# Q, K and V of five of eight pairs of column groups from seven block products in place of eight

## The chip, the cores and the metric

The kernel runs on one core of a Trainium2 chip. The metric is the device time of one execution in microseconds. Five engines work at once, each in its own order: TensorE (PE, matmuls; its weight loads, PEld, overlap them), VectorE (DVE), ScalarE (ACT), GpSimd (POOL) and SyncE (SP, which issues most of the transfers). Matmuls write to PSUM, whose banks DVE and ACT read.

## The reference

One transformer block with two parallel branches on a normalized input, S = 2048 rows of D = 576, hidden size F = 4608, H = 32 heads of 18:

```python
xn = _layernorm(x, axis=-1)
return x + _A_ref(xn, A_wqkv, A_wo) + _B_ref(xn, B_w1, B_b1, B_w2, B_b2)
```

`_A_ref` computes q, k and v = xn @ wqkv, attends from each position to the 8 positions at distance 0, 2, ..., 14 behind it (softmax over those that exist), and multiplies by wo. `_B_ref` is a feed-forward network: h = relu(xn @ w1 + b1), squared, times w2, plus b2.

## The kernel before

The rows are cut into NB = 4 blocks of TB = 512. All matmuls take F32R operands. For accuracy each operand is split into a rounded part (hi) and the remainder (lo), and hi·hi, hi·lo and lo·hi are summed in PSUM. D = 576 is four chunks of 128 and a last one of 64; the last chunk's hi and lo lie on top of each other in one fifth tile of 128 partitions, so it needs two matmuls and not three.

The work is written out in steps. There are NT = 144, 36 in each block, one for each slice of 128 of F. Step n loads the weights of slice n + 2 (`load_w`), splits w1 of slice n + 1 (`split_w1`: an ACT copy L118 to w1h, a DVE subtraction L120 to w1l), runs what `pre` lists for the step, then `ffn1(n)` (14 matmuls L492 of 512 columns into a bank of PSUM; Relu L494 and two Squares L497 and L498 on ACT, the remainder hl on DVE L499), `split_w2(n)` (L124, L126), what `mid` lists, two pieces of side work, `ffn2(n - 2)` (14 matmuls L515 into five banks that stay open for the whole block), and a third piece. The order in which an engine's instructions really stand is chosen at build time by a scheduler that works through the program in that order of priority; only the opening and the tail are written by hand (`manual_schedule`). `issue_after` puts what an engine gets in its block behind a given instruction of that engine.

Q, K and V of a block are made in four groups of columns (8 heads each: 144 columns of K, 144 of V, and some of Q). In blocks 1 to 3 the groups have 512, 512, 384 and 320 columns (`WIDE`), in block 0 448, 512, 384 and 384; always 1728 in all. `load_wq` loads a group's five chunks of weights and splits them (L118, L120, 10 instructions on each of two tiles `wqh`, `wql`). `qkv` then runs, for each of NJ = 4 slices of 128 rows, 14 matmuls (`three`, L372; in block 0's first group L236) into a bank `wk` of which there are three, and copies Q, K and V out with three ACT copies (L393 to L395). `qkv_close` sends K and V to memory and gets the 14 rows before the block back. Matmuls L372 have the x part as the stationary and the weights as the moving operand.

`attention(b, g)` is side work on DVE in 19 pieces (products L425 and L447, sums L428 and L451 to L453, small operations L435 to L442), then a write to memory and a gather (`ob`). `o_chunk` and `o_acc` in steps 29 to 37 of a block transpose the result and multiply it by wo into the open banks; they need all four groups. `layernorm` (statistics L138, a power on POOL L147) and `normalize` (L334 and a split) prepare the next block's x, which `load_x` has loaded in two layouts, rows (`xb`) and transposed (`xt`). `load_residual` loads x again (`xr`), to which `finish` adds the open banks at a block's end. In before, block b's four groups start in steps -2, 4, 11 and 18 of the block (9, 15 and 20 in block 0), with their weights three or four steps earlier. All loads and stores but the opening's two are issued by SP.

Of the kernel before, what the change touches and what calls it, by code (L numbers as in the profile page):

```python
# [43 lines left out]
def block_kernel(ctx: ExitStack, tc: tile.TileContext, x, xt, wqkv, wo, w1, b1, w2, b2, out):  # L44
# [5 lines left out]
    pw = ctx.enter_context(tc.tile_pool(name="pw", bufs=3, space=bass.MemoryType.PSUM))  # L50
# [39 lines left out]
    yp = {}  # L90

    def load_x(b):
        xb[b] = sb.tile([P, NJ, D], F32, name="xb", bufs=1)
        with tc.issue_after(last_load[0].ins):
            nc.sync.dma_start(xb[b], xv[b])
            xT[b] = sb.tile([P, NC, TB], F32, name="xt", bufs=1)
            nc.sync.dma_start(xT[b], xt[b])

    def load_first():
        xb[0] = sb.tile([P, NJ, D], F32, name="xb", bufs=1)  # L100
        raw = sb.tile([P, NC, TB], F32, name="xr", bufs=1)[:, :, :WIDE[0][0]]
        hi = mt.tile([P, NC, WQ], F32R, name="wqh")[:, :, :WIDE[0][0]]
        lo = mt.tile([P, NC, WQ], F32R, name="wql")[:, :, :WIDE[0][0]]
        nc.sync.dma_start(xb[0][:, 0, :288], xv[0, :, 0, :288])  # L104
        nc.scalar.dma_start(xb[0][:, 0, 288:], xv[0, :, 0, 288:])
        nc.scalar.dma_start(raw[:, 0], wqkv[0, 0, :, 0, :WIDE[0][0]])
        nc.sync.dma_start(xb[0][:, 1], xv[0, :, 1])
        for c in range(1, NC):
            nc.sync.dma_start(raw[:, c], wqkv[0, 0, :, c, :WIDE[0][0]])
# [19 lines left out]
    ln, last_load, last_hl = {}, [None], [None]  # L129
# [61 lines left out]
    def open_rows():  # L191
# [36 lines left out]
        def part(j, i):  # L228
# [3 lines left out]
            if (0, j) not in qp:  # L232
                qp[0, j] = pw.tile([P, TB], F32, name="wk")
                done[j] = 0
            done[j] += 1
            nc.tensor.matmul(qp[0, j][:, :WIDE[0][0]], (xl if a == 1 else xh)[0][:, c, js], (lo if a == 2 else hi)[:, c],  # L236
# [109 lines left out]
    def load_residual(b):  # L346
        xr[b] = sb.tile([P, NC, TB], F32, name="xr", bufs=1)
        nc.sync.dma_start(xr[b][:, :NC - 1], xt[b, :, :NC - 1])
        nc.sync.dma_start(xr[b][:D - DM, NC - 1], xt[b, :D - DM, NC - 1])
# [3 lines left out]

    def load_wq(b, g):
        n = WIDE[b][g]
        hi = mt.tile([P, NC, WQ], F32R, name="wqh")[:, :, :n]
        lo = mt.tile([P, NC, WQ], F32R, name="wql")[:, :, :n]
        for c in range(NC):
            r = sb.tile([P, n], F32, name="wqr", bufs=2)
            nc.sync.dma_start(r, wqkv[min(b, 1), g, :, c, :n])  # L360
# [3 lines left out]
    kv, attended = {}, set()  # L364
# [10 lines left out]

    def qkv_open(b, g, w):
        if g == 0:
            qo[b] = sb.tile([P, NJ, D], F32, name="qo", bufs=1)
            ob[b] = sb.tile([P, NJ * G, CG], F32, name="ob", bufs=1)
# [3 lines left out]
    def qkv_rows(b, g, j):  # L383
        hi, lo = qw[g]
        p = qp[g, j] = pw.tile([P, TB], F32, name="wk")
        js = slice(j * P, (j + 1) * P)
        three(p[:, :WIDE[b][g]], lambda c: xh[b][:, c, js], lambda c: xl[b][:, c, js],
# [281 lines left out]
    def step(n):  # L669
# [21 lines left out]
        if not busy:  # L691
            piece()
# [50 lines left out]
```

## Time and profile before

| What | us |
|---|---|
| time, median of 3 runs | 1161.33 (1161.21 to 1161.37) |
| the profiled execution's own time | 1161.42 |
| its span, first to last instruction | 1159.7 |
| PE busy | 1154.3 |
| DVE busy | 847.5 |
| ACT busy | 602.2 |
| POOL busy | 18.3 |
| transfers: 185.90 MB, mean 160 GB/s, 16 engines busy | 50.4% |

A profile row for a group of instructions reads: line, engine, operation, output tile <- input tiles, shapes, xcount, then busy time in us and the mean of one in ns, then the idle time of the engine just before them and what ended it. A row by form gives shortest, median and longest duration in ns and the first and last start. A row of the chain in time, or of a timeline, begins with start and duration in us. A row of waits reads: waiting engine and line <- engine and line waited for, us in total, times, longest. A row by stretch gives its ends, its length, the busy us (and instructions) of PE, PEld, DVE, ACT and POOL, then TensorE's granted clock, the share of the DMA engines' time and GB/s. A row of transfers gives the tile, the issuing queue, the count, KB of one, and the median us from issue to landing.

### The profile page before, as it was taken

The numbers are of one execution on the slowest core, as the hardware profiler recorded it, in microseconds if no ns is written. First come the engines' busy times: TensorE is split into PE (matmuls) and PEld (weight loads), VectorE is DVE, ScalarE is ACT, GpSimd is POOL, SyncE is SP. The second block draws the span as 40 slices with busy tenths as digits, with TensorE's granted clock in tenths as the row PEclk, the third lists the DMA queues.
The fourth block names the chain that finished last, engine by engine and source line by source line (L and its number), as shares of the span: only waits on it lengthen the run. The fifth ranks groups of instructions, "written<-read, shape, count | busy, mean of one in ns | idle before, by whom it ended". The sixth has DMA issues, their size and how long they took to land.

```text
span 1159.7 us, 14795 instructions
## 1 busy us (share of the span) xinstructions
PE 1154.3 (100%) x5227; PEld 966.5 (83%) x5227; DVE 847.5 (73%) x1373; ACT 602.2 (52%) x1086; POOL 18.3 (2%) x32
## 2 busy tenths in 40 slices
PE   9999999999999999999999999999999999999998
PEld 7888888888888888888888888888888888888887
DVE  6967798892788686995287969698528795957453
ACT  7645545563545454555364546555535455545552
POOL 2000000000000100000000010000000000000000
PEclk9999999999999999999999999999999999999999
DMA  8656547432656655444266665644326645353421
GB/s 290 214 170 223 177 133 234 123 112 63 209 190 206 212 183 198 132 115 120 63 234 203 203 216 153 214 111 125 106 75 232 221 131 184 108 181 111 121 63 51
DMA packets 89674, 185.90 MB, mean 160 GB/s; under 512 B 9984, under 2 KB 33280, under 8 KB 88320
## 3 DMA queue, kind: packets, MB, share of 16 engines
q1 hardware_dynamic: 89312, 184.58, 50.1%
q8 instruction: 41, 0.67, 0.2%
q10 hardware_dynamic: 288, 0.38, 0.1%
q14 instruction: 33, 0.27, 0.1%
HBM read 165.96 MB, written 18.96 MB: 159 GB/s over the span
## 4 chain that ended last, share of the span: by engine, by line
PE 99%; DMA 0%; DVE 0%; SPq 0%; issue 0%
PE y L515 44%; PE wk L492 39%; PE wk L372 14%; PE wk L236 1%; DMA xb<-in_x 0%; PE y L172 0%; PE wk L564 0%; DVE st L138 0%; DVE xr L566 0%; SPq L104 0%; DVE xt L166 0%
## 5 line engine op out<-in xcount | busy, mean ns | idle before, releaser
L515 PE MATMUL y<-hh,w2s 128*128 128x512 f32 x1292 | 319.8, 389 | 0.0
L515 PEld LDWEIGHTS y<-hh,w2s 128*128 128x128 f32 x1292 | 242.5, 188 | 50.4
L492 PE MATMUL wk<-xh,w1h 128*128 128x512 f32 x720 | 210.3, 389 | 0.0
L515 PE MATMUL y<-hl,w2s 128*128 128x512 f32 x718 | 189.5, 389 | 0.0
L492 PE MATMUL wk<-xh,w1l 128*128 128x512 f32 x720 | 187.6, 389 | 0.0
L120 DVE TENSOR_TENSOR w1l<-raw,w1h 128x640 fp32r<-128x640 f32 x144 | 118.1, 820 | 66.4 <-ACT w1h L118 52.0
L118 ACT ACTIVATE w1h<-raw 128x640 fp32r<-128x640 f32 x144 | 106.1, 737 | 115.7 <-PE wk L492 114.0
L124 ACT ACTIVATE w2s<-raw 128x576 fp32r<-128x576 f32 x144 | 97.8, 683 | 120.0 <-PE y L515 118.1
L492 PEld LDWEIGHTS wk<-xh,w1l 128*128 128x128 f32 x720 | 135.1, 188 | 28.1
L515 PEld LDWEIGHTS y<-hl,w2s 128*128 128x128 f32 x718 | 134.8, 188 | 28.0
L492 PEld LDWEIGHTS wk<-xh,w1h 128*128 128x128 f32 x720 | 134.9, 188 | 27.5
L492 PE MATMUL wk<-xl,w1h 128*128 128x512 f32 x576 | 154.1, 389 | 0.0
L126 DVE TENSOR_TENSOR w2s<-raw,w2s 128x512 fp32r<-128x512 f32 (+1 forms) x288 | 118.0, 453 | 47.3 <-ACT w2s L124 46.2
L499 DVE TENSOR_TENSOR hl<-r,hh 128x512 fp32r<-128x512 f32 x144 | 98.8, 686 | 42.4 <-ACT r L498 42.3
L492 PEld LDWEIGHTS wk<-xl,w1h 128*128 128x128 f32 x576 | 108.1, 188 | 22.6
L494 ACT ACTIVATE r<-wk,b1t 128x512 f32<-128x512 f32 x144 | 98.5, 684 | 39.7 <-PE wk L492 39.4
L425 DVE TENSOR_TENSOR pr<-qo,kv 128x1152 f32<-128x1152 f32 x64 | 86.6, 1353 | 34.7 <-DMA kv<-kscr 34.7
L372 PE MATMUL wk<-wqh,xh 128*128 128x512 f32 (+2 forms) x300 | 106.3, 355 | 0.0
L372 PE MATMUL wk<-wql,xh 128*128 128x512 f32 (+2 forms) x300 | 106.3, 355 | 0.0
L498 ACT ACTIVATE r<-r 128x512 f32<-128x512 f32 x144 | 91.0, 632 | 4.4
L497 ACT ACTIVATE hh<-r 128x512 fp32r<-128x512 f32 x144 | 90.9, 632 | 4.1
L447 DVE TENSOR_TENSOR pr<-lg,kv 128x1152 f32<-128x1152 f32 x64 | 86.8, 1356 | 1.6
(91 smaller groups left out, 961.1 us busy)
## 6 DMA issues: line engine op xcount, KB each, us to landing
raw<-in_w SPq DMA_DIRECT2D x144, 320.0 KB, 3.0
raw<-in_w SPq DMA_DIRECT2D x144, 288.0 KB, 2.8
kv<-kscr SPq DMA_DIRECT2D x16, 1008.0 KB, 5.7
kv<-vscr SPq DMA_DIRECT2D x16, 1008.0 KB, 8.2
wqr<-in_wqkv SPq DMA_DIRECT2D x35, 256.0 KB, 3.3
raw<-in_wo SPq DMA_DIRECT2D x20, 288.0 KB, 2.8
wqr<-in_wqkv SPq DMA_DIRECT2D x25, 192.0 KB, 4.0
kscr<-kv SPq DMA_DIRECT2D x16, 288.0 KB, 3.0
```

The source lines that it names most:

```text
L118: i = nc.scalar.activation(hi, raw, AF.Copy)
L120: i = nc.vector.tensor_tensor(out=lo, in0=raw, in1=hi.bitcast(F32), op=ALU.subtract)
L124: nc.scalar.activation(w[:, :D], raw, AF.Copy)
L126: nc.vector.tensor_tensor(out=w[:, o:o + n], in0=raw[:, a:a + n], in1=w[:, a:a + n].bitcast(F32), op=ALU.subtract)
L372: nc.tensor.matmul(ps, l, r, start=i == 0, stop=i == len(mm) - 1)
L447: nc.vector.tensor_tensor(out=pr.rearrange("p w (a d) -> p w a d", d=DH), in0=at[:, :, :, None].to_broadcast([P, W, HG, DH]), in1=shifted( ...
L492: nc.tensor.matmul(p, l, r, start=i == 0, stop=i == len(mm) - 1)
L494: nc.scalar.activation(r, p, AF.Relu, bias=b1t[:, f:f + 1])
L497: nc.scalar.activation(hh, r, AF.Square)
L498: nc.scalar.activation(r, r, AF.Square)
L499: last_hl[0] = nc.vector.tensor_tensor(out=hl, in0=r, in1=hh.bitcast(F32), op=ALU.subtract)
L515: nc.tensor.matmul(yp[b][c], v, a, start=first and c not in cs[:i], stop=c in last and c not in cs[i + 1:], skip_group_check=True)
```

## The change

Groups 0 and 1 form pair 0, groups 2 and 3 pair 1; in a pair both groups now have 432 columns (`PAIR`). Block 0 is made as before. In block 1 pair 0, in blocks 2 and 3 both pairs are made with seven block products (Winograd's form of Strassen's scheme). The four full chunks make two halves of the inner dimension, the 512 rows two halves of 256, the pair's two groups two halves of the columns. A product (`multiply`) takes sums of parts of x and sums of parts of the weights over two chunks: 2 x 3 matmuls for each of two slices of 128 rows. The fifth chunk isn't part of the scheme; products 2, 7, 4 and 3 carry two more matmuls a slice for it (`EXTRA`). Products 1 and 2, products 6, 7 and 4, and products 5 and 3 each accumulate in the same two banks (`qk`); after each product its state is copied (ACT, products 1 and 2) or added to a kept result (DVE, the others): K and V to `cst`, which takes the place of `xb`, and Q to `qo`.

The sums of x for products 6, 7, 5 and 3 are made on DVE from the normalized `xT`, rounded by ACT and the remainder taken by DVE (`sums`, tile `sx`). The sums of weights are made once, pair 0's in block 0 from step 6 and pair 1's in block 1 from step 13 of the block (`preparation`): quarters of the weights are loaded through POOL's queue into `xt` and `xr` while these are free, POOL subtracts (`minus`), ACT rounds, POOL takes the remainder and stores both to memory (`emit`: 17 a pair). In block 0 one is made each step, in block 1 three in two steps. `load_product` gets one product's weights from memory two steps ahead, through POOL's queue, into `wqh` and `wql` in turn, and the fifth chunk's sums into the end of that tile and into `wqr`.

One product is made each step: pair 0 of block 1 in steps 42 to 48, of blocks 2 and 3 in steps -6 to 0 of the block, pair 1 in steps 3 to 9. In these steps `ffn1` uses the bank `wk` alone (`held`); else it goes through the three banks as before (`bank`). Groups 2 and 3 of block 1 are made as before, in steps -2 and 3 of the block, with 432 columns. `fetch` then gets a group's K and V whole from memory and starts its attention: in steps 13 and 18 of block 1, and 1, 6, 11 and 16 of blocks 2 and 3. The transposed x is loaded 14 steps ahead of a block in place of 26, the rows 25; normalization starts 12 steps ahead, or 11, and then goes before the other side work. The residual is loaded in step 34, 68, and 13 of blocks 2 and 3. From step 19 on every odd step has a fourth piece of side work.

```diff
-WIDE = [(448, 512, 384, 384)] + 3 * [(512, 512, 384, 320)]
-QAT = [[sum(n - 2 * CG for n in w[:g]) for g in range(G + 1)] for w in WIDE]
+WIDE = (448, 512, 384, 384)
+QAT = [sum(n - 2 * CG for n in WIDE[:g]) for g in range(G + 1)]
+PAIR = (432, 432)
+QP = (0, 288)
+PREP = (6, 13)
...
+    turns, held = [0], set()
+
+    def bank(own=False):
+        turns[0] += not own
+        if own or turns[0] % 3 == 0:
+            return pw.tile([P, TB], F32, name="wk")
+        return pw.tile([P, TB], F32, name="qk", bufs=2)
...
+    def load_xt(b):
+        xT[b] = sb.tile([P, NC, TB], F32, name="xt", bufs=1)
...
+    def columns(b, g):
+        if b:
+            p, h = divmod(g, 2)
+            n = PAIR[p]
+            q = QP[p] + h * (n - 2 * CG)
+            return n, q, lambda c: wpair[p, :, c, h, :n]
+        n = WIDE[g]
+        return n, QAT[g], lambda c: wqkv[g, :, c, :n]
...
+    def minus(out, a, b):
+        nc.gpsimd.tensor_tensor(out=out, in0=a, in1=b, op=ALU.subtract)
+
+    def emit(raw, dst, n):
+        outs[0] += 1
+        o = mt.tile([P, 2, n], F32R, name=("wos", "sx", "wqh", "wql")[outs[0] % (2 if outs[0] < 18 else 4)], bufs=1)
+        split(o[:, 0], o[:, 1], raw, nc.scalar)
+        minus(o[:, 1], raw, o[:, 0].bitcast(F32))
+        nc.gpsimd.dma_start(dst, o.bitcast(F32))
+
+    quarters = {}
+
+    def load_quarter(p, m, c, h):
+        n = PAIR[p]
+        if c < 4:
+            k, home = 2 * (c // 2) + h, "xt" if m == p else "xr"
+        else:
+            k, home = 4, "xr" if h else "xt"
+        if (p, home) not in quarters:
+            quarters[p, home] = sb.tile([P, NC, TB], F32, name=home, bufs=1).rearrange("p c t -> p (c t)")
+        v = quarters[p, c, h] = quarters[p, home][:, k * n:(k + 1) * n]
+        i = nc.gpsimd.tensor_copy(v[:, :1], gate[0][:, :1].bitcast(F32))
+        with tc.issue_after(i.ins):
+            nc.gpsimd.dma_start(v, wpair[p, :, c, h, :n])
+
+    def preparation(p):
+        b = lambda c, h: quarters[p, c, h]
+        n = PAIR[p]
+        for m in (p, 1 - p):
+            for i, c, h, minuend in ((1, 0, 0, None), (2, 2, 0, None), (3, 2, 1, None), (5, 0, 0, (0, 1)), (7, 0, 1, (2, 1)),
+                                     (6, 2, 1, (0, 0)), (4, 2, 0, (2, 1))):
+                c += m
+                if i == 5:
+                    minus(b(c, h), b(m, 1), b(c, h))
+                elif i == 7:
+                    minus(b(c, h), b(2 + m, 1), b(c, h))
+                elif i == 6:
+                    minus(b(c, h), b(c, h), b(m, 0))
+                elif i == 4:
+                    minus(b(c, h), b(c, h), b(2 + m, 1))
+                emit(b(c, h), wm[p][i - 1][:, 2 * m:2 * m + 2], n)
+                yield
+            if m == p:
+                for h in (1, 0):
+                    emit(b(4, h), we[p][h], n)
+                    yield
+                minus(b(4, 1), b(4, 0), b(4, 1))
+                emit(b(4, 1), we[p][2], n)
+                yield
+
+    EXTRA = {2: 0, 7: 1, 4: 2, 3: 1}
+    mw, sx, qk, cst = {}, {}, {}, {}
+
+    def load_product(b, p, i, k):
+        n = PAIR[p]
+        t = mt.tile([P, NC, WQ], F32R, name=("wqh", "wql")[k % 2]).rearrange("p c t -> p (c t)")
+        w = t[:, :4 * n].rearrange("p (c t) -> p c t", c=4)
+        nc.gpsimd.dma_start(w, wm[p][i - 1])
+        hi = lo = None
+        if i in EXTRA:
+            hi = t[:, 4 * n:5 * n]
+            lo = sb.tile([P, n], F32R, name="wqr", bufs=2)
+            nc.gpsimd.dma_start(hi, we[p][EXTRA[i]][:, 0])
+            nc.gpsimd.dma_start(lo, we[p][EXTRA[i]][:, 1])
+        mw[i] = w, hi, lo
+
+    HALF = TB // 2
+
+    def sums(b, i):
+        v = lambda k, t: xT[b][:, 2 * k:2 * k + 2, t * HALF:(t + 1) * HALF]
+        s = sx[i] = mt.tile([P, 4, HALF], F32R, name="sx")
+        lo = s[:, 2:]
+        f = sb.tile([P, TB], F32, name="r", bufs=3).rearrange("p (c t) -> p c t", c=2)
+
+        def tt(out, a, b, op):
+            nc.vector.tensor_tensor(out=out, in0=a, in1=b, op=op)
+
+        if i == 7:
+            tt(f, v(0, 0), v(0, 1), ALU.subtract)
+        else:
+            tt(f, v(0, 1), v(1, 1), ALU.add)
+            if i != 5:
+                tt(f, f, v(0, 0), ALU.subtract)
+            if i == 3:
+                tt(f, v(1, 0), f, ALU.subtract)
+        nc.scalar.activation(s[:, :2], f, AF.Copy)
+        tt(lo, f, s[:, :2].bitcast(F32), ALU.subtract)
+
+    def result(b, p, t, row, col):
+        j = 2 * row + t
+        n = PAIR[p]
+        q = QP[p] + col * (n - 2 * CG)
+        return cst[b, p][:, col, :, j], qo[b][:, j, q:q + n - 2 * CG]
+
+    def halves(a, n):
+        return a[:, :2 * CG].rearrange("p (k c) -> p k c", k=2), a[:, 2 * CG:n]
+
+    def multiply(b, p, i):
+        n = PAIR[p]
+        if i == 1:
+            cst[b, p] = sb.tile([P, 2, 2, NJ, CG], F32, name="xb", bufs=1)
+            results(b)
+        w, ehi, elo = mw.pop(i)
+        s = sx.pop(i, None)
+        first = i in (1, 6, 5)
+        for t in range(2):
+            if first:
+                qk[t] = pw.tile([P, TB], F32, name="qk", bufs=2)
+            at = slice(t * P, (t + 1) * P)
+            if s is None:
+                k, row = {1: (0, 0), 2: (1, 0), 4: (1, 1)}[i]
+                js = slice(row * HALF + t * P, row * HALF + (t + 1) * P)
+                a = lambda m: (xh[b][:, 2 * k + m, js], xl[b][:, 2 * k + m, js])
+            else:
+                a = lambda m: (s[:, m, at], s[:, 2 + m, at])
+            mm = []
+            for m in range(2):
+                hi, lo = a(m)
+                mm += [(hi, w[:, 2 * m]), (hi, w[:, 2 * m + 1]), (lo, w[:, 2 * m])]
+            if i in EXTRA:
+                row = {2: 0, 7: 1, 4: 1, 3: 0}[i]
+                js = slice(row * HALF + t * P, row * HALF + (t + 1) * P)
+                mm += [(xh[b][:, NC - 1, js], ehi), (xh[b][:, NC - 1, js], elo)]
+            for c, (l, r) in enumerate(mm):
+                nc.tensor.matmul(qk[t][:, :n], l, r, start=first and c == 0, stop=c == len(mm) - 1,
+                                 skip_group_check=True)
+        for t in range(2):
+            src = halves(qk[t], n)
+            kept = result(b, p, t, 1, 0)
+            row, col = {1: (1, 0), 2: (0, 0), 6: (0, 1), 7: (1, 1), 4: (1, 0), 5: (1, 1), 3: (0, 1)}[i]
+            for o, a, u in zip(result(b, p, t, row, col), src, kept):
+                if i in (1, 2):
+                    nc.scalar.activation(o, a, AF.Copy)
+                else:
+                    nc.vector.tensor_tensor(out=o, in0=a, in1=u if i in (6, 7, 4) else o, op=ALU.add)
+        if i in (4, 3):
+            h = (4, 3).index(i)
+            for k, scr in enumerate((kscr, vscr)):
+                nc.sync.dma_start(flat(scr[2 * p + h], (PAD + b * TB) * CG, [NJ * CG, P], NJ * CG),
+                                  cst[b, p][:, h, k].rearrange("p j c -> p (j c)"))
+
+    def fetch(b, g):
+        kv[g] = tuple(mt.tile([P, NE, CG], F32, name="kv", bufs=3) for _ in range(2))
+        for t, scr in zip(kv[g], (kscr[g], vscr[g])):
+            nc.sync.dma_start(t.rearrange("p e c -> p (e c)"),
+                              flat(scr, (PAD + b * TB - HALO) * CG, [NJ * CG, P], NE * CG))
+        side.append(attention(b, g))
...
-        p = pw.tile([P, TB], F32, name="wk")
+        p = bank(own=n in held)
...
+    prep = []
+
+    def next_difference():
+        while prep:
+            try:
+                with tc.issue_after(last_square[0].ins):
+                    next(prep[0])
+                return
+            except StopIteration:
+                prep.pop(0)
 
     def at(where, n, f, *a):
         where.setdefault(n, []).append((f, a))
...
     for b in range(NB):
         n0 = b * NF
         if b:
-            at(pre, n0 - 26, load_x, b)
+            at(pre, n0 - 25, load_x, b)
             at(pre, n0 - 22, lambda b=b: side.insert(0, layernorm(b)))
-            at(pre, n0 - 12, lambda b=b: side.append(normalize(b)))
-            at(pre, n0 - 6, load_wq, b, 0)
-        at(pre, n0 + 13, load_residual, b)
-        if b:
-            at(pre, n0 - 2, start, b, 0)
-        for g, n in ((1, 4), (2, 11), (3, 18)) if b else ((1, 9), (2, 15), (3, 20)):
-            at(pre, n0 + n - 3, load_wq, b, g)
-            at(pre, n0 + n, start, b, g)
+            at(pre, n0 - 14, load_xt, b)
+            at(pre, n0 - (12 if b < 2 else 11), lambda b=b: side.insert(0 if b > 1 else len(side), normalize(b)))
+            for p, a in enumerate((n0 - 6, n0 + 3) if b > 1 else (n0 + 6,)):
+                for k, i in enumerate((1, 2, 6, 7, 4, 5, 3)):
+                    at(pre, a + k - 2, load_product, b, p, i, k)
+                    if i in (6, 7, 5, 3):
+                        at(mid, a + k - 1, sums, b, i)
+                    at(pre, a + k, multiply, b, p, i)
+                    held.add(a + k)
+            for g, n in enumerate((1, 6, 11, 16) if b > 1 else (13, 18)):
+                at(pre, n0 + n, fetch, b, g)
+            if b < 2:
+                for g, l, n in ((2, -6, -2), (3, 1, 3)):
+                    at(pre, n0 + l, load_wq, b, g)
+                    at(pre, n0 + n, start, b, g)
+            at(pre, n0 + (13 if b > 1 else 32), load_residual, b)
+        else:
+            at(pre, 34, load_residual, b)
+            for g, n in ((1, 9), (2, 15), (3, 20)):
+                at(pre, n - 3, load_wq, b, g)
+                at(pre, n, start, b, g)
+        if b < 2:
+            a = n0 + PREP[b]
+            at(mid, a, lambda p=b: prep.append(preparation(p)))
+            when = lambda k: a + (k * 2 // 3 if b else k)
+            for k in range(17):
+                at(mid, when(k), next_difference)
+            for k, m in ((0, b), (10, 1 - b)):
+                for i, (c, h) in enumerate(((m, 0), (2 + m, 0), (2 + m, 1), (m, 1))):
+                    at(pre, when(k + i) - 3, load_quarter, b, m, c, h)
+            for i, h in enumerate((1, 0)):
+                at(pre, when(7 + i) - 3, load_quarter, b, b, NC - 1, h)
...
+            if n > 18 and n % 2:
+                piece()
```

More of the change, by code (lines that the diff above doesn't have):

```diff
@@ L90, in block_kernel @@
     yp = {}
+    turns, held = [0], set()
[4 more added lines that the diff above has]
+        return pw.tile([P, TB], F32, name="qk", bufs=2)
+    wm = [[dram.tile([P, 4, n], F32, name=f"wm{p}{i}") for i in range(7)] for p, n in enumerate(PAIR)]
+    we = [[dram.tile([P, 2, n], F32, name=f"we{p}{i}") for i in range(3)] for p, n in enumerate(PAIR)]
     def load_x(b):
@@ L384, in qkv_rows @@
         hi, lo = qw[g]
-        p = qp[g, j] = pw.tile([P, TB], F32, name="wk")
+        p = qp[g, j] = bank()
         js = slice(j * P, (j + 1) * P)
-        three(p[:, :WIDE[b][g]], lambda c: xh[b][:, c, js], lambda c: xl[b][:, c, js],
+        three(p[:, :columns(b, g)[0]], lambda c: xh[b][:, c, js], lambda c: xl[b][:, c, js],
               lambda c: hi[:, c], lambda c: lo[:, c])
@@ L577, in o_chunk @@
     def o_chunk(b, c):
-        assert b in attended
+        assert attended.count(b) == G
         if c == 0:
@@ L614, in block_kernel @@
     nc.vector.memset(warm, 0.0)
-    wp = pw.tile([P, TB], F32, name="wk")
+    wp = bank()
     def warm_up(n, width=TB, after=None):
@@ L726 @@
         "wqkv": wqkv,
+        "wpair": wpair,
         "wo": wo,
```

71 lines of the change are left out of this document (41 added, 30 removed).

## The prediction

> **What bounds the kernel now.** I read the head of the page and its chain of waits first, then the chain in order of time, then what TensorE (PE) itself waited for.
>
> ```profile
> span 1159.7 us, 14795 instructions
> PE 1154.3 (100%) x5227; PEld 966.5 (83%) x5227; DVE 847.5 (73%) x1373; ACT 602.2 (52%) x1086; POOL 18.3 (2%) x32
> PE 99%; DMA 0%; DVE 0%; SPq 0%; issue 0%
> PE y L515 44%; PE wk L492 39%; PE wk L372 14%; PE wk L236 1%; DMA xb<-in_x 0%; PE y L172 0%; PE wk L564 0%; DVE st L138 0%; DVE xr L566 0%; SPq L104 0%; DVE xt L166 0%
> 71.78 12.69 PE wk L372 x56
> 122.55 9.73 PE wk L372 x56
> 439.51 8.21 PE wk L372 x56
> 1116.15 6.35 PE y L515 x28
> PE wk L621 <- DVE warm L614: 1.2, 1, 1.2
> PE wk L619 <- POOL rs L147: 0.6, 1, 0.6
> PE y L172 <- DVE xt L166: 0.2, 1, 0.2
> ```
>
> The reader is to see one engine from end to end. The chain is 99% PE, and the last three rows are all that PE's matmuls waited for in the whole execution: 2.0 us, all in the opening. So each matmul taken out is worth its own duration, as long as no other engine or transfer becomes late. The four rows of the chain in time give that duration: 12.69/56 = 0.2266 us at 512 columns, 9.73/56 = 0.1738 at 384, 8.21/56 = 0.1466 at 320; 6.35/28 = 0.2268 in the feed-forward part, whose 28 matmuls make a step of 6.35 us. From 320 to 512 columns the price grows by 0.000417 us a column, so 432 columns cost 0.1466 + 112 x 0.000417 = 0.1933 us. By one rate for all columns it would lie between 432/512 x 0.2266 = 0.1912 and 432/384 x 0.1738 = 0.1955.
>
> **What the change removes from PE.** Two groups were 2 x 4 x 14 = 112 matmuls. A pair of them is now seven products of 2 x 6, and four of the seven carry 2 x 2 more for the fifth chunk: 84 + 16 = 100. Blocks 2 and 3 went from 56 x (2 x 0.2266 + 0.1738 + 0.1466) = 43.3 us to 200 x 0.1933 = 38.7; block 1 keeps two direct groups of 432 columns: 100 + 112 matmuls, 41.0 us. Saved: 4.66 + 4.66 + 2.33 = **11.65 us** (60 matmuls; 11.5 to 11.7 with the bounds of the price). The new order of banks adds no matmul, and the output drains and the tail aren't touched.
>
> **What it adds beside PE.** Durations are from the groups of instructions, some with shapes apart:
>
> ```profile
> L120 DVE TENSOR_TENSOR w1l<-raw,w1h 128x640 fp32r<-128x640 f32 x144 | 118.1, 820 | 66.4 <-ACT w1h L118 52.0 <-PE wk L492 11.4 <-ACT lg L438 2.6
> L126 DVE TENSOR_TENSOR w2s<-raw,w2s 128x512 fp32r<-128x512 f32 (+1 forms) x288 | 118.0, 453 | 47.3 <-ACT w2s L124 46.2
> L499 DVE TENSOR_TENSOR hl<-r,hh 128x512 fp32r<-128x512 f32 x144 | 98.8, 686 | 42.4 <-ACT r L498 42.3
> L118 ACT ACTIVATE w1h<-raw 128x640 fp32r<-128x640 f32 x144 | 106.1, 737 | 115.7 <-PE wk L492 114.0 <-DMA wqr<-in_wqkv 1.4 <-DMA raw<-in_w 0.3
> L494 ACT ACTIVATE r<-wk,b1t 128x512 f32<-128x512 f32 x144 | 98.5, 684 | 39.7 <-PE wk L492 39.4
> L447 DVE TENSOR_TENSOR pr<-lg,kv 128x1152 f32<-128x1152 f32 x64 | 86.8, 1356 | 1.6
> L425 DVE TENSOR_TENSOR pr<-qo,kv 128x1152 f32<-128x1152 f32 x64 | 86.6, 1353 | 34.7 <-DMA kv<-kscr 34.7
> L428 DVE TENSOR_REDUCE lg<-pr 128x64 f32<-128x1152 f32 x64 | 86.2, 1347 | 0.0
> L451 DVE TENSOR_TENSOR pr<-pr 128x576 f32<-128x576 f32 x64 | 48.1, 752 | 0.5
> L452 DVE TENSOR_TENSOR pr<-pr 128x288 f32<-128x288 f32 x64 | 29.1, 455 | 1.4
> L453 DVE TENSOR_TENSOR qo<-pr 128x144 f32<-128x144 f32 x64 | 19.5, 305 | 1.4
> L442 DVE TENSOR_TENSOR lg<-lg,sm 128x256 f32<-128x256 f32 x16 | 6.8, 425 | 0.6
> L441 DVE RECIPROCAL sm<-sm 128x32 f32<-128x32 f32 x16 | 5.6, 353 | 0.6
> L120 DVE TENSOR_TENSOR wql<-wqr,wqh 128x512 fp32r<-128x512 f32 (+2 forms) x75 | 44.1, 602 | 47.2 <-ACT wqh L118 47.1
> L118 ACT ACTIVATE wqh<-wqr 128x512 fp32r<-128x512 f32 (+2 forms) x75 | 40.6, 561 | 87.7 <-DMA wqr<-in_wqkv 58.1 <-PE wk L372 29.3
> L334 DVE TENSOR_TENSOR xt<-xt,mb 128x512 f32<-128x512 f32 x30 | 33.0, 1154 | 0.0
> L120 DVE TENSOR_TENSOR xl<-xt,xh 128x512 fp32r<-128x512 f32 x12 | 8.2, 710 | 0.0
> L138 DVE BATCH_NORM_STATS2 st<-xb 128x6 f32<-128x288 f32 x32 | 12.3, 447 | 10.3 <-DMA xb<-in_x 10.3
> ```
>
> VectorE (DVE), per pair: the sums of x are 11 operations of 128x512 (3 + 2 + 2 + 4), 11 x 0.686 = 7.5 us; five products are added to kept results, 5 x 2 x (0.455 + 0.305) = 7.6 us by L452 and L453. Ten splits of weights go, 10 x 44.1/75 = 5.9 us. Net 9.2 us, 46 us over five pairs: 847.5 becomes about 894 of 1150, still below PE. In a product step it fits: the 2.41 us that every step needs (0.820 + 2 x 0.453 + 0.686), 15.1/7 = 2.2 for the product, and 3.5 pieces of attention (one attention is four times the six L425 to L453 rows, 22.3, and five small operations between L441 and L442, 2.0: 24.3 us in 19 pieces, 1.28 each) make 9.05 us; PE's step is 6.35 + 14.3 x 0.1933 = 9.11. A bank is read again one step later, so its additions (1.5 us) have 6.35 us. The feed-forward part has one bank of its own in those steps, which Relu (0.684 us) must have read within the 3.17 + 2.76 us to the next use. I cost all of it at nothing; without that cover PE waits for whatever DVE or ACT is behind.
>
> ScalarE (ACT) loses more than it gains per pair (ten splits and 24 copies against eight narrower copies and four roundings) and gets 34 roundings of weights in blocks 0 and 1, 34 x 40.6/75 = 18 us: nothing, at 52% busy. They are queued behind a step's last Square, so what stands behind one that has to wait is the next weight split, which then keeps PE's next step.
>
> **The transfers.** 35 loads of 864 KB (five pairs of seven), 40 of 216 KB, and in blocks 0 and 1 54 loads and stores of quarters and sums go through POOL's queue, which carried no load before. Bounds from the SP queue:
>
> ```profile
> kv<-vscr SPq DMA_DIRECT2D x16, 1008.0 KB, 8.2
> wqr<-in_wqkv SPq DMA_DIRECT2D x15, 160.0 KB, 6.4
> xt<-in_xt SPq DMA_DIRECT2D x3, 1280.0 KB, 8.0
> ```
>
> A product's weights are issued when the product two earlier has read its buffer, and have 6.35 + 2.76 + 6.35 = 15.5 us. In parallel they need some 8 us (1,296 KB by the third row): hidden. One after the other, by the slower rows, 8.2 + 6.4 + 6.4 = 21 us: late by 5.5. I take the first end, since in all rows size adds little to a landing time of some 3 to 8 us. The two transfers moved by the change are x transposed (load_xt now two or three steps ahead of its use, 12.7 us against 8.0) and the residual (step 34 for a drain in step 37): both hidden; on SP's queue each now stands behind the feed-forward weights of its step. On POOL's queue a product's load waits for PE with only the next loads behind it, as the layer norm's powers and the subtractions fall in other steps. The K and V of the fetched groups now come whole from memory, some 8 us after the step that asks; attention starts later by that, and nothing on PE waits for its start.
>
> **The place where it is tight** is block 1, steps 49 to 66. Attention for groups 0 and 1 can't start before step 49 now, and must feed the output projection in step 67; the same steps hold layer norm and normalization of block 2, and the preparation of pair 1 on GpSimd (POOL). DVE in 17 steps: 17 x 2.41 = 41.0; two attentions 48.6; layer norm 5.4 (8 x 0.447 and small ones); normalization 15.1 (10 x 1.154, 5 x 0.710); first weights and chunk of the projection 2.3 (2 x 0.453, 2 x 0.686): 112.4 us. PE in the same steps: 17 x 6.35 = 107.9. DVE may fall behind by the lead of the next step's w1l, which PE reads 9 matmuls into it: 6.35 + 2.04 - 0.737 - 0.820 = 6.8 us. So 112.4 against 114.7: just covered, but the preparation isn't in it yet.
>
> The preparation is 26 POOL subtractions a block (17 remainders, 9 differences). The trace has two of that kind:
>
> ```profile
> L203 POOL TENSOR_TENSOR wql<-xr,wqh x2: 1147/1151/1155, 9.1 to 11.3; 128x448 fp32r<-128x448 f32 x2
> L203 DVE TENSOR_TENSOR wql<-xr,wqh x3: 618/652/967, 8.4 to 12.8; 128x448 fp32r<-128x448 f32 x3
> 9.41 0.82 DVE L138 BATCH_NORM_STATS2 st<-xb 128x6 f32<-128x288 f32 x2
> 11.26 1.16 POOL L203 TENSOR_TENSOR wql<-xr,wqh 128x448 fp32r<-128x448 f32 x1
> 11.93 1.54 DVE L203 TENSOR_TENSOR wql<-xr,wqh 128x448 fp32r<-128x448 f32 x2
> ```
>
> The first DVE operation of the last row began at 11.93, beside POOL's until 12.42 (0.49 us), and is the one of 0.967; the other two took 0.635 on average. So it lost 0.33 us of 0.49 shared. Over the two POOL operations that is 0.17 us each, and 26 x 0.17 = 4.3 us for a block: 112.4 + 4.3 - 114.7 = **2.0 us** of PE waiting in block 1. Bounds: 0, if POOL falls into DVE's gaps; 26 x 1.15 x 0.33/0.49 = 20 us lost, 18 us of waiting, if DVE always wants in. I take 2.0, since the trace has DVE work of many kinds beside POOL and only some of it slowed. In block 0 the same costs nothing by this row, even at 20 us:
>
> ```profile
> 50.00:178.00 128.00, 128.00 (x593) 109.25 (x592) 102.20 (x175) 64.35 (x128) 2.66 (x4) 1.00 0.54 171
> ```
>
> The third busy time is DVE's: 25.8 us of 128 free.
>
> **The sum.** The profiled execution took 1161.42 us (span 1159.7), 0.09 above the median of 1161.33. 1161.33 - 11.65 + 2.0 = **1151.7 us**.
>
> **The rivals.**
> *DVE locked out by POOL.* The place is block 1's preparation, the price 0.78 us of DVE for each POOL subtraction, 20 us in all; it decides against the change once DVE loses more than 14 us there (11.65 + 2.3 spare). For it: the 0.967 row, and some 80% of DVE's time (all but the reductions and layer norm) goes to operations on two tiles in SBUF, like that one. Against it: two bn_stats ran in 0.82 us beside the first POOL subtraction, against 0.447 for one on average, and POOL has idle steps in which to lag. Time: 1149.7 + 18 = 1167 us.
> The Trainium skill (SBUF — State Buffer, Who interferes with whom) states the rule behind this rival: a DVE instruction with two SBUF inputs contends with a GpSimd instruction that reads SBUF, and the later one is blocked until the first has finished. By that rule the 0.967 would have been 0.49 + 0.635 = 1.13; the row shows two thirds of it.
> *Everything is hidden.* The 6.8 us of lead and list order absorb block 1: 1149.7 us. For it: in the present trace PE doesn't wait once after the opening, though normalization comes as a burst of 15 us of DVE in two steps. Against it: no stretch now has DVE above 100% of PE, and block 1 will.
> *The weights come late.* If POOL's queue moves a product's three loads one after the other, the 20 products with a fifth chunk are each 5.5 us late: 1149.7 + 110 = 1260 us. For it: no row shows POOL's queue at such a load. Against it: the sizes and the 15.5 us.
> *It doesn't do what it says* would be PE at the old 112 matmuls a pair; the loop over products excludes it.
>
> **How the numbers follow.** The forecast, with some 1 to 7 us of waiting (1150.5 to 1156.5): 0.47. Everything hidden (1149 to 1150.5): 0.27. Locked out (1158 to 1171): 0.18, about half of it below 1165. Weights late, or additions late in product steps: 0.08. The range 1149 to 1165 holds 0.47 + 0.27 + 0.09 = 0.83. A difference under 0.2% (2.3 us) can't be told from none. Faster than 1159: the first two and a little of the third, 0.75; within 1159 to 1163.7: 0.05, from the third; slower: 0.20, the rest of the third and the fourth.
>
> **What will show it.** Right: some 60 matmuls fewer, 500 of them of 432 columns at 0.19 us; DVE near 895 us and POOL near 80; what PE waits for lies between steps 49 and 66 (400 to 520 us into the span) and names DVE. The lock: DVE operations of 0.68 us reading 1 us and more beside POOL's. Late weights: PE waiting for a DMA from the sums at the start of products. Wrong altogether: PE waits spread over blocks 2 and 3, where I count none.

## The result, and the profile after

The changed kernel took 1175.55 us (median of 4 runs, 1171.79 to 1176.26) against 1161.35 before: a ratio of 1.0116, with an interval of 1.0094 to 1.0137. It is slower, where 1151.7 was forecast. The profiled execution is the fastest of the four (1171.79 us, span 1170.1).

From its page, first busy times and the chain by engine, then the groups that answer to those of before:

```profile
span 1170.1 us, 14971 instructions
PE 1151.5 (98%) x5167; PEld 966.1 (83%) x5167; DVE 924.8 (79%) x1478; ACT 587.6 (50%) x1010; POOL 167.8 (14%) x233
PE 75%; DVE 14%; DMA 6%; issue 4%; ACT 1%; SPq 0%; POOL 0%; DVEq 0%; POOLq 0%
L136 DVE TENSOR_TENSOR w1l<-raw,w1h 128x640 fp32r<-128x640 f32 x144 | 123.9, 861 | 66.5 <-ACT w1h L134 59.1
L142 DVE TENSOR_TENSOR w2s<-raw,w2s 128x512 fp32r<-128x512 f32 (+1 forms) x288 | 125.8, 478 | 52.3 <-ACT w2s L140 51.5
L682 DVE TENSOR_TENSOR hl<-r,hh 128x512 fp32r<-128x512 f32 x144 | 107.3, 745 | 35.7 <-ACT r L681 35.7
```

The 60 matmuls are gone (5227 to 5167). But the chain, 99% PE before, is now 75% PE and 14% DVE, and the same DVE instructions on the same shapes have become longer: w1l 820 to 861 ns, hl 686 to 745 ns. A mean hides where, so here are stretches of 10 us of the changed kernel (columns: stretch, length, busy us and instructions of PE, PEld, DVE, ACT, POOL; granted clock; DMA share; GB/s) and the forms of DVE's operations between 440 and 525 us:

```profile
240.00:250.00 10.00, 8.74 (x39) 6.91 (x38) 10.00 (x15) 4.09 (x7) 0.00 (x0) 1.00 0.30 81
250.00:260.00 10.00, 7.53 (x34) 5.91 (x33) 8.49 (x16) 9.90 (x18) 0.00 (x0) 1.00 0.41 139
460.00:470.00 10.00, 8.09 (x36) 6.38 (x34) 9.93 (x8) 6.45 (x12) 9.56 (x13) 1.00 0.71 255
470.00:480.00 10.00, 8.78 (x26) 7.01 (x27) 9.93 (x11) 3.83 (x6) 3.94 (x4) 0.66 0.64 228
500.00:510.00 10.00, 7.01 (x29) 5.13 (x29) 9.90 (x12) 4.31 (x8) 5.54 (x8) 1.00 0.91 304
530.00:540.00 10.00, 8.31 (x37) 6.52 (x36) 7.75 (x13) 4.60 (x8) 0.00 (x0) 1.00 0.31 97
```

```profile
L682 DVE TENSOR_TENSOR hl<-r,hh 128x512 fp32r<-128x512 f32 x11 | 11.8, 1074 | 0.0
L142 DVE TENSOR_TENSOR w2s<-raw,w2s 128x64 fp32r<-128x64 f32 x12 | 6.4, 535 | 0.0
L635 DVE TENSOR_TENSOR pr<-pr 128x288 f32<-128x288 f32 x8 | 6.2, 778 | 0.0
L611 DVE TENSOR_REDUCE lg<-pr 128x64 f32<-128x1152 f32 x4 | 5.4, 1345 | 0.0
```

PE is short of work mainly in two places: 240 to 260 us, after block 0's preparation, and 460 to 540 us, in block 1's. In the second DVE shows 9.9 us busy in 10, yet only 8 to 12 instructions. Operations on two tiles in SBUF take far longer than before (hl 686 to 1074 ns, the small w2s 218 to 535, the 288-wide sum 455 to 778); the reduction L611, with one input, keeps its 1345 ns. The timeline shows one case:

```profile
457.81 2.84 DVE L682 TENSOR_TENSOR hl<-r,hh 128x512 fp32r<-128x512 f32 x1
457.90 1.11 POOL L449 TENSOR_TENSOR wos<-xt,wos 128x432 fp32r<-128x432 f32 x1
458.99 1.12 POOL L449 TENSOR_TENSOR sx<-xr,sx 128x432 fp32r<-128x432 f32 x1
462.72 2.20 PE L699 MATMUL y<-hh,w2s 128*128 128x512 f32 x9
467.71 0.39 PE L675 MATMUL wk<-xh,w1h 128*128 128x512 f32 x1
468.99 2.18 DVE L136 TENSOR_TENSOR w1l<-raw,w1h 128x640 fp32r<-128x640 f32 x1
471.22 2.50 PE L675 MATMUL wk<-xh,w1l 128*128 128x512 f32 x5 [3.13 <-DVE w1l L136]
473.52 3.94 PE L699 MATMUL y<-hh,w2s 128*128 128x512 f32 x9
```

hl began at 457.81 and ended at 460.65, after two GpSimd subtractions one behind the other. 0.69 us of its own and the 2.21 of theirs make 2.90; it took 2.84. Later PE waits 3.13 us for a w1l that took 2.18, and then runs at half speed: the same nine matmuls that took 2.20 us take 3.94. That is the clock of 0.66 in the stretch from 470.

To see where time is lost I set the start of Relu in a step beside that of the same step before (from the timelines, us). Step 33 lies behind block 0's preparation, 65 behind block 1, 97 and 133 behind blocks 2 and 3. Negative is ahead. The last column is the median time.

| kernel | 33 | 65 | 97 | 133 | time |
|---|---|---|---|---|---|
| before, the start itself | 265.89 | 521.92 | 781.99 | 1068.59 | 1161.35 |
| after | +7.2 | +20.7 | +14.2 | +10.2 | 1175.6 |
| e1 memsets in place of subtractions | -0.2 | -1.7 | -5.7 | -9.7 | 1152.0 |
| e8 copies in place of subtractions | 0.0 | -1.6 | -5.5 | -9.5 | 1152.1 |
| e12 memsets in block 0 only | -0.1 | +12.8 | +6.3 | +2.3 | 1163.9 |
| e13 memsets in block 1 only | +9.7 | +8.2 | +4.2 | +0.2 | 1161.8 |
| e7 normalization thinner | +7.6 | +20.9 | +13.7 | +9.7 | 1171.3 |
| e2 subtractions on DVE | -4.4 | +2.8 | +3.9 | -0.1 | 1161.5 |
| e3 block 1 direct | +9.5 | +25.0 | +19.4 | +15.4 | 1177.3 |
| e5 block 1 direct, preparation spread | +6.7 | +21.3 | +15.1 | +11.1 | 1174.0 |
| e6 as e5, on DVE | -3.7 | +8.1 | +7.0 | +3.0 | 1163.7 |
| e9 as e6, normalization thinner | -4.1 | +5.5 | -1.5 | -5.5 | 1156.5 |
| e10 five pairs, on DVE, thinner | +0.3 | +1.1 | -4.1 | -8.1 | 1155.5 |

A mark also moves when the build-time order puts other work behind the step and not before it: PE has the same work up to step 33 in every row, and yet e2, e6 and e9 are some 4 us ahead there. So a mark inside a block is good to some 4 us; from 97 to 133 every row gains the same 4.0. Against e1, which has the same matmuls, after is 7.4 us behind at step 33 and 19.9 at 97 and at 133: it loses 7.4 us in block 0, where PE's own work is that of before, and 12.5 in block 1. Blocks 2 and 3, with the products of four pairs, win 8.0 in e1 (9.7 - 1.7). The times of e1, e2, e3, e7, e8, e12 and e13 are single executions; a kernel with many subtractions on GpSimd varies by some 5 us.

### The profile page after: what moved, and what is told of

Its sections match the earlier page's. It is cut to its first block, busy times and chain, and to the rows that moved or that the text cites. A ratio compares the mean times of both kernels' runs of the same rounds, so it can differ in the third digit from the quotient of the medians.

```text
span 1170.1 us, 14971 instructions
## 1 busy us (share of the span) xinstructions
PE 1151.5 (98%) x5167; PEld 966.1 (83%) x5167; DVE 924.8 (79%) x1478; ACT 587.6 (50%) x1010; POOL 167.8 (14%) x233
## 4 chain that ended last, share of the span: by engine, by line
PE 75%; DVE 14%; DMA 6%; issue 4%; ACT 1%; SPq 0%; POOL 0%; DVEq 0%; POOLq 0%
PE y L699 34%; PE wk L675 16%; PE qk L675 13%; PE qk L572 8%; PE qk L398 2%; DVE w1l L136 2%; DVE w2s L142 2%; DVE pr L630 2%; DVE lg L611 2%; DVE pr L608 1%; DMA xb<-in_x 1%; DVE pr L634 1%; DMA kv<-vscr 1%; PE wk L398 1%; DMA wqr<-in_wqkv 1%
## 5 line engine op out<-in xcount | busy, mean ns | idle before, releaser
L682 DVE TENSOR_TENSOR hl<-r,hh 128x512 fp32r<-128x512 f32 x144 | 107.3, 745 | 35.7 <-ACT r L681 35.7
L675 PE MATMUL wk<-xh,w1h 128*128 128x512 f32 x360 | 106.2, 390 | 0.0
L675 PE MATMUL qk<-xh,w1h 128*128 128x512 f32 x360 | 105.1, 389 | 0.0
L675 PE MATMUL wk<-xh,w1l 128*128 128x512 f32 x360 | 95.2, 393 | 4.4 <-DVE w1l L136 4.4
L675 PE MATMUL qk<-xh,w1l 128*128 128x512 f32 x360 | 93.7, 390 | 2.5 <-DVE w1l L136 2.4
L611 DVE TENSOR_REDUCE lg<-pr 128x64 f32<-128x1152 f32 x64 | 86.2, 1346 | 0.1
L675 PEld LDWEIGHTS wk<-xh,w1l 128*128 128x128 f32 x360 | 68.0, 190 | 19.3 <-DVE w1l L136 5.4
L675 PEld LDWEIGHTS qk<-xh,w1l 128*128 128x128 f32 x360 | 67.3, 188 | 17.7 <-DVE w1l L136 3.8
L675 PEld LDWEIGHTS qk<-xh,w1h 128*128 128x128 f32 x360 | 67.6, 188 | 13.8
L675 PEld LDWEIGHTS wk<-xh,w1h 128*128 128x128 f32 x360 | 67.6, 188 | 13.0
```

Of the source, the lines that this page charges most:

```text
L611: nc.vector.tensor_reduce(out=lg[:, j * HG:(j + 1) * HG].rearrange("p a w -> p w a"), in_=pr.rearrange("p w (a d) -> p w a d", d=DH), axis ...
L675: nc.tensor.matmul(p, l, r, start=i == 0, stop=i == len(mm) - 1)
L682: last_hl[0] = nc.vector.tensor_tensor(out=hl, in0=r, in1=hh.bitcast(F32), op=ALU.subtract)
```

## The experiments

**What GpSimd's subtractions do.** The kernel e1 keeps every transfer and ACT operation and has memsets where the 52 subtractions were.

```diff
 def minus(out, a, b):
-    nc.gpsimd.tensor_tensor(out=out, in0=a, in1=b, op=ALU.subtract)
+    for _ in range(2):
+        nc.gpsimd.memset(out.bitcast(F32), 0.0)
```

> The changed kernel, but each of GpSimd's 52 subtractions is two memsets of the same tile: as many GpSimd instructions and transfers, but none of them reads SBUF (remainders and differences of the weights are zero). Lock theory (a GpSimd subtraction keeps DVE's operations with two SBUF inputs out for its whole time, 31 us in all): DVE falls from 925 to about 895 us, hl back to 0.69 us everywhere, the 7 us lost by step 33 and most of the 17 us lost in block 1 are gone, 1150 to 1155 us. Demand theory (block 1's steps 49 to 66 ask more of DVE than PE takes, with or without GpSimd): block 0 recovers 7 us, block 1 still loses 10 us and more, 1161 to 1168 us. Transfers on POOL's queue as the cause: no change, 1172 to 1176.

1151.95 us. Busy times, one group, and all that PE's matmuls waited for:

```profile
PE 1144.6 (100%) x5167; PEld 964.7 (84%) x5167; DVE 886.3 (77%) x1478; ACT 591.2 (51%) x1010; POOL 143.8 (12%) x285
L683 DVE TENSOR_TENSOR hl<-r,hh x144: 624/687/732, 28.0 to 1137.1; 128x512 fp32r<-128x512 f32 x144
PE qk L806 <- DVE warm L799: 1.3, 1, 1.3
PE qk L804 <- POOL rs L163: 0.6, 1, 0.6
PE y L188 <- DVE xt L182: 0.2, 1, 0.2
```

POOL is almost as busy as in after, but PE waits for nothing outside the opening, and no hl takes over 732 ns (after: 2841 at most). DVE lost 924.8 - 886.3 = 38.5 us, 0.74 us for each of 52 subtractions. The demand theory and the transfers fall: block 1's late attention stands in this kernel too, and costs nothing.

e8 has `nc.gpsimd.tensor_copy(out, a)` there instead, one tile read and one written.

> The changed kernel, but each GpSimd subtraction is a copy of its first operand: it reads one tile and writes one (remainders and differences of the weights are wrong). If any GpSimd instruction that reads SBUF holds DVE out, DVE's w1l and hl are longer than their 0.82 and 0.69 us in blocks 0 and 1, by less than with two operands since a copy is shorter: DVE 890 to 910 us, 1153 to 1165. If only the second operand counts, as with memsets: DVE 886 us, about 1152.

1152.12 us.

```profile
PE 1144.7 (100%) x5167; PEld 964.8 (84%) x5167; DVE 896.0 (78%) x1478; ACT 590.7 (51%) x1010; POOL 138.1 (12%) x233
L449 POOL COPY xr<-xr 128x432 f32<-128x432 f32 x8 | 7.0, 872 | 0.6 <-DMA xr<-in_wpair 0.5
```

DVE lost 9.7 us, 0.19 for each copy of 0.87 us: a reader of one tile holds DVE too, but much less, and PE had lead enough for it.

e12 and e13 put the memsets into one block's preparation each.

> The changed kernel, GpSimd's subtractions replaced by two memsets in block 0's preparation only (pair 0's remainders and differences are zero). Lock theory: the 7 us lost by step 33 are gone, block 1's loss of some 17 us stays: 1164 to 1169. If the two losses share one cause that either half removes: under 1160.

> The same in block 1's preparation only (pair 1's remainders and differences are zero). Lock theory: the 7 us of block 0 stay and block 1 loses 2 us or less: 1156 to 1161, and with the other half the two savings add up to the 20 us and more that both together saved. Demand theory: block 1 still loses 10 us: 1166 to 1172.

1163.92 and 1161.82 us. In e12 block 0's loss is gone (-0.1) and block 1 still loses 12.9; in e13 block 0 loses 9.7 and block 1 nothing. 2.3 of the 9.7 us are lost in e13's opening, before the first subtraction (its step 2 is already 2.3 us late), which also puts its time 0.8 above the expectation; 7.4 are left for block 0, as in after. Against the profiled 1171.8 the two win 7.9 and 10.0, both together 19.8: the losses add up (17.9, or 20.2 without e13's opening, against 19.8).

**More room for the preparation.** e3 makes block 1 as before, so that its attention is early again; e5 also spreads the preparations.

```diff
-            for p, a in enumerate((n0 - 6, n0 + 3) if b > 1 else (n0 + 6,)):
+            for p, a in enumerate((n0 - 6, n0 + 3) if b > 1 else ()):
...
-                for g, l, n in ((2, -6, -2), (3, 1, 3)):
+                for g, l, n in ((0, -6, -2), (1, 1, 4), (2, 8, 11), (3, 15, 18)):
...
-PREP = (6, 13)
+PREP = (6, 4)
...
-            when = lambda k: a + (k * 2 // 3 if b else k)
+            when = lambda k: a + (k * 3 // 2 if b else k * 4 // 3)
```

The first two changes are e3 (and `emit` with two tiles in turn, wos and sx; `fetch` for blocks 2 and 3 alone), all four e5.

> The changed kernel with block 1 made as before (groups in steps -2, 4, 11, 18 with 512... now 432 columns each, attention early again), so four of eight pairs with products; the preparation keeps its steps and GpSimd. PE should save 9.3 us against the kernel before. Lock theory: block 0 still loses 7 us, block 1 loses part of what GpSimd takes (13 us less the gaps of early attention), 1159 to 1168. Demand theory: block 1's loss is gone, only block 0's 7 us remain, 1158 to 1160.

> As e3, and the preparation is spread: pair 0's 17 sums over 22 steps of block 0 (before: 17), pair 1's over 25 steps of block 1 from its step 4 (before: 11 steps from step 13). Lock theory: the same 31 us of DVE fall into DVE's free time, so both losses shrink, 1152 to 1158, faster than the kernel before. Demand theory: as e3, 1152 to 1160. If GpSimd's subtractions cost by their number and not by what DVE has free, 1159 and more.

1177.26 and 1174.00 us (ratio for e5 1.0116, 1.0093 to 1.0139). e3 misses its ranges, and e5 those of both theories; what came is its third case, 1159 and more. With four pairs, early attention and more steps for the preparations (22 in place of 17, 25 in place of 11), block 0 of e5 still loses 6.7 us by the marks and block 1 14.6. So room on average isn't what decides. The timeline of e5 in block 1:

```profile
519.22 3.25 DVE L350 TENSOR_TENSOR xt<-xt,mb 128x512 f32<-128x512 f32 x3
522.74 2.19 DVE L350 TENSOR_TENSOR xt<-xt,mb 128x512 f32<-128x512 f32 x2
525.56 2.11 DVE L350 TENSOR_TENSOR xt<-xt,mb 128x512 f32<-128x512 f32 x2
528.40 9.49 POOL L449 TENSOR_TENSOR sx<-xr,sx 128x432 fp32r<-128x432 f32 x1 [15.90 <-ACT sx L134]
529.67 2.50 PE L675 MATMUL qk<-xh,w1l 128*128 128x512 f32 x5 [4.94 <-DVE w1l L136]
```

PE waits 4.94 us for a w1l that stands on DVE behind a burst of normalization (L350). DVE came late to that burst. And the exclusion works both ways: a subtraction of 1.15 us took 9.49 on GpSimd while DVE ran one two-input operation after the other.

**The same subtractions on DVE** (`nc.vector.tensor_tensor` in `minus`), in the changed kernel (e2) and in e5 (e6).

> The changed kernel with the 52 subtractions on DVE in place of GpSimd. Lock theory: DVE does in its own 52 x 0.6 = 31 us what it lost by waiting, so about the same time, 1166 to 1176; a little less than the change if the build-time order, which now sees the cost, places them better. Transfers as the cause: no change, 1172 to 1176. If one GpSimd subtraction costs DVE much more than its own 0.6 us, clearly faster, under 1166.

> As the run with block 1 direct and the preparation spread, with the 52 subtractions on DVE in place of GpSimd. PE should save 9.3 us against the kernel before. If what that run lost is GpSimd holding DVE (a subtraction there costs DVE more than doing it itself, 0.6 us), it is faster than it by 10 us and more: 1153 to 1161, faster than the kernel before. If what it lost is only that DVE has too much to do around normalization, about as that run, 1168 to 1175.

e2 1161.49 us, e6 1163.66 (ratio 1.0025, 1.0016 to 1.0035): faster than with GpSimd by 10 us and more, e6 short of its expectation. From e6's page and groups:

```profile
PE 1151.7 (99%) x5179; PEld 969.7 (83%) x5179; DVE 901.4 (78%) x1509; ACT 596.7 (51%) x1032; POOL 86.3 (7%) x166
L449 DVE TENSOR_TENSOR sx<-xr,sx 128x432 fp32r<-128x432 f32 x9 | 5.4, 600 | 0.0
```

and from e2's page:

```profile
PE 1148.0 (99%) x5167; PEld 965.8 (83%) x5167; DVE 909.2 (78%) x1530; ACT 591.8 (51%) x1010; POOL 101.7 (9%) x181
```

DVE makes all 52 subtractions here, at 0.60 us each, and is still busy less than with GpSimd: 901.4 us against 909.6 in e5, 909.2 against 924.8 in after. So a subtraction handed to GpSimd costs DVE more than doing it itself. Taking 52 x 0.60 = 31 us off e6's 901.4, DVE lost some 39 us in e5, 0.76 a subtraction (an estimate: the subtractions of e2 add only 23 us to e1's 886.3). How much of the 10 us in time comes from the build-time order, which now sees these operations on DVE, isn't separated.

Beyond the opening, PE waits just twice in e6, once in block 0 and once in block 1, and neither time for w1l:

```profile
255.00 1.30 DVE L769 STREAM_TRANSPOSE r<-ob 128x512 f32<-128x512 f32 x2 [5.36 <-DMA ob<-o]
256.42 5.01 PE L699 MATMUL y<-kv,wos 128*128 128x512 f32 x14 [3.19 <-ACT kv L134]
539.18 0.71 DVE L769 STREAM_TRANSPOSE r<-ob 128x512 f32<-128x512 f32 x1 [6.44 <-DMA ob<-o]
539.93 0.63 ACT L134 ACTIVATE kv<-r 128x512 fp32r<-128x512 f32 x1 [7.34 <-DVE r L769]
541.66 0.66 PE L572 MATMUL qk<-wql,xh 128*128 128x432 f32 x2 [2.94 <-ACT qo L580]
```

DVE stands idle for the gather of attention's last group (ob), and ACT behind DVE; in block 1 the copies of a product (L580) stand behind that on ACT. DVE's last sum of attention (L636) began at 246.5 and 527.8 us, after normalization's last L350 (242.1 and 522.6).

**The burst.** One empty piece behind each of normalization's five, in the changed kernel (e7), in e6 (e9), with five pairs on DVE (e10), and in the kernel before (e14); two empty pieces in e15.

```diff
                     nc.vector.tensor_tensor(out=hi[64:], in0=xT[b][64:, c], in1=t[64:].bitcast(F32), op=ALU.subtract)
             yield
+            yield
```

> The changed kernel, but each of normalization's five pieces is followed by an empty piece, so its 15 us of DVE come over about three steps in place of one and a half. Burst theory (GpSimd takes DVE's time all along, but PE only waits where normalization also uses up the lead of w1l): the losses by step 33 and by step 66 shrink by 5 us and more together, 1160 to 1168. If PE's waiting follows GpSimd alone: 1170 to 1176 as the change.

> As the run with block 1 direct, the preparation spread and the subtractions on DVE, with the thinner normalization as well. Burst theory: a few us less than without the empty pieces, 1152 to 1156. Without a burst effect: the same within 1 us.

> The changed kernel (five pairs, preparation in its own steps) with the subtractions on DVE and the thinner normalization. Without GpSimd, subtractions on DVE alone gave 1161.5. Burst theory: normalization's burst was what remained, so 1153 to 1158. If what remained there is the demand of block 1 (attention from step 49 on, 112 us of DVE and now 16 more in 108 us of PE), 1159 to 1162.

> The best kernel so far (four pairs, subtractions on DVE, preparation spread, thinner normalization), with pair 1's preparation over 22 steps in place of 25, so that it ends in step 61, where normalization of block 2 begins, and not in step 64. Burst theory: less waiting between steps 62 and 66, 1153 to 1156. If the overlap of the two plays no part: 1156 to 1157.5 as before.

> The kernel before with the thinner normalization alone (an empty piece after each of its five). If the gain of the faster kernels comes from the products: no change, 1161.3 within 0.5 us, since PE waits for nothing there. If the thinner normalization is a gain by itself: 1156 to 1159.

> Five pairs, the subtractions on DVE, and two empty pieces after each piece of normalization in place of one. Burst theory: what is left above 1152 is still the burst, so 1151 to 1155. If the rest is DVE's whole demand: 1154 to 1158 as before.

- e9: 1156.49 us, ratio 0.9959 (0.9944 to 0.9974), 7 us less than e6 and half a us above its expectation. Attention's last sum now begins at 243.7 and 522.7 us, 2.8 and 5.1 earlier, and the two waits for what follows it are gone; one of 1.4 us for w1l is left. So the burst does cost e6 time, but by what it delays in attention, not by the lead of w1l, of which the theory spoke.
- e10: 1155.53 us, ratio 0.9956 (0.9940 to 0.9973), 6 us less than e2. With e9 it is faster than both kernels of this study.
- e7: 1171.26 us in one execution, within the range for waiting that follows GpSimd alone; after's own runs begin at 1171.79. The 5 us expected didn't come, and the marks at 33 and 65 are after's: beside GpSimd's subtractions the thinner normalization gains nothing that one execution shows.
- e14: 1161.38 us, ratio 0.9998 (0.9989 to 1.0008). The thinner normalization alone is worth nothing, so the gain of e9 and e10 is that of the products.
- e15: 1156.98 us, ratio 0.9963 (0.9949 to 0.9977), no better than e10: what is left there isn't the burst. Its longest wait of PE, 2.4 us, again comes behind a wait for the gather ob (DVE 5.79 us, ACT 6.52).
- e11 (e9, with `k * 4 // 3` for both blocks): 1159.74 us, ratio 0.9984 (0.9975 to 0.9993), 3 us slower than e9 and not faster. Its PE waited 2.0 us for copies of a product's Q that e9 had in time. They stood on ACT behind 5.46 us of waiting for the gather ob, as in e6; attention's last sum began at 525.2 us (e9: 522.7). Why the shorter preparation makes attention late is open.

## Why the prediction was wrong

**What failed** is the size of one term. The prediction took "0.17 us each, and 26 x 0.17 = 4.3 us for a block", the mean of two GpSimd operations in the trace of before. Measured: 0.74 us for each of the 52. One of the two had run beside bn_stats, which reads one tile (the reduction L611, with one tile too, kept its 1345 ns beside the subtractions); the other had shared only 0.49 of its 1.16 us with exposed work. Averaging the two brought the price to about a quarter of the 0.78 us that the other gives by itself, 0.33 us lost of 0.49 shared: 20 us for a block, near the 19 measured. "Some of it slowed" was read as an average, where the forms of the slowed operation told which work is exposed; 80% of DVE's time was named as exposed in the rival, and not used in the sum.

The Trainium skill (SBUF — State Buffer, Who interferes with whom) was nearer: the later instruction is blocked until the first has finished. In size the trace of after agrees: hl took 2.84 us, and its own 0.69 with the 2.21 of both subtractions make 2.90. In order it doesn't: hl's record starts first (457.81 against 457.90 us), and it was held through both all the same. The Trainium skill also says that an instruction of GpSimd that only writes doesn't contend, and e1 bears that out (hl at most 0.73 us).

**The second failure** is "in block 0 the same costs nothing even at 20 us", from 25.8 us of DVE free in 128. Block 0 lost 7.4 us against e1, and e12 shows that the subtractions caused it. PE waited 1.7 us for ACT between 150 and 200 us, and twice at 240 to 260 us, when GpSimd had long finished (0.00 us busy from 210 us on):

```profile
243.44 1.43 PE L675 MATMUL wk<-xh,w1l 128*128 128x512 f32 x5 [1.26 <-DVE w1l L136]
250.00 0.64 ACT L356 ACTIVATE xh<-xt 64x512 fp32r<-64x512 f32 x1 [5.48 <-DVE xt L350]
253.70 3.47 PE L699 MATMUL y<-kv,wos 128*128 128x512 f32 x14 [2.47 <-ACT kv L134]
```

In e1 ACT's operation L356, which waits for normalization, starts at 241.22 us, 8.8 us earlier. So DVE's free time in the stretch hadn't made up for the delay: normalization's 15 us found DVE late, w1l came late behind them, and the first copy for the output projection (kv) behind ACT's wait for them. The burst is where PE had to wait, but spreading it took nothing off block 0's loss in e7's one execution (+7.6 at step 33), while taking GpSimd's subtractions out there did (e12).

**The rival that came true** is DVE locked out by POOL (0.18). Its 20 us of DVE for block 1 fit (38.5 for two blocks). Its time of 1167 is too low: in the profiled run, at 1171.8, block 1 cost 12.5 us and not 18, but block 0 cost 7.4 and not nothing, and the change saved 10 and not 11.65. That two of these errors partly cancel is luck. What the other three runs lost beyond it, 3 to 4.5 us, no trace shows.

**The saving** was mis-sized too: 11.65 us, of which about 10 came. The chain in time of e1 shows one product, with its fifth chunk, of block 2:

```profile
568.09 3.13 PE qk L573 x16
```

3.13/16 = 0.196 us for 432 columns, the upper bound given (0.1955), not 0.1933. With it blocks 2 and 3 save 43.3 - 200 x 0.196 = 4.1 us each and block 1 1.8 (212 matmuls): 10.0, and e1 is ahead by 9.7 in step 133. The bounds stated for the saving, 11.5 to 11.7, don't follow from the bounds of the price either: with 0.1955 the same sum gives 10.2, with 0.1912 12.9.

**What was right.** 60 matmuls fewer. DVE without the lock 886 us (894 said), and ACT fell, from 602.2 to 587.6. (POOL, forecast near 80, came out at 167.8: issuing its 129 transfers takes 0.55 us each, 71 us, which the forecast left out, and the subtractions took 73 us and not 60.) The weights of the products aren't late, through POOL's queue and in parallel:

```profile
wqh<-wm POOLq DMA_DIRECT2D x20, 864.0 KB, 5.9
wqr<-we POOLq DMA_DIRECT2D x20, 216.0 KB, 5.6
```

The tight place, steps 49 to 66, was right for block 1; so was that late attention alone doesn't overfill it (e1, e13). That everything else is hidden (1149.7) is what e1 shows, at 1152.

## What to carry to other kernels

Work handed from a busy VectorE to GpSimd isn't off VectorE if it reads two tiles there: here one subtraction cost VectorE 0.74 us, and doing it itself 0.60. Before pricing such a move, sort VectorE's work by how many tiles it reads from SBUF, and take a price only from rows beside exposed work. And free time summed over a stretch doesn't pay for a delay: look for the next burst in order, and ask what it makes late.

## What the runs showed of the hardware

- The exclusion is mutual and can starve either side: GpSimd subtractions of 1.1 us took up to 3.3 us in after and 9.49 in e5; DVE's hl of 0.69 took up to 2.84.
- A wait of PE of 3.13 us (468.1 to 471.2) was followed by matmuls at half speed: nine in 3.94 us and not 2.20, granted clock 0.66 over that 10 us. The 26 matmuls between 471.2 and 480 were busy 8.78 us, 5.9 at the usual 0.227 each: 2.9 us lost, nearly as much as the wait. In e2 a wait of 2.16 us was followed by 14 matmuls in 5.07 us, while after's of 2.47 us was followed by 14 in 3.47; at the usual price they take 3.17.
- A copy on GpSimd, one tile read, cost DVE 0.19 us for 0.87 of its own; a memset nothing that shows.
